# Running maxima by scalar columns on VectorE, h scaled out of PSUM, output in two alternating tiles

## The chip, the core and the metric

The kernel runs on one core of a Trainium2 chip. A core has a matrix engine (TensorE, "PE" in the profile; its weight loads are "PEld"), three engines for elementwise work (VectorE "DVE", ScalarE "ACT", GpSimd "POOL") and a queue that only issues transfers (SyncE "SP"). Each works through its own list of instructions in order, and they wait for one another by semaphores. SBUF is the working memory with 128 partitions; TensorE writes into PSUM, which has eight banks per partition. The metric is the device time of one execution in microseconds (us); the median of three is compared.

## The reference, cut to what matters

Two stages are chained: attention through 32 inducing points, and a channel mix. x has 4 batches of 12608 tokens of 128 channels.

```python
def mab(q, kv):
    s = scale * (q @ kv.transpose(0, 2, 1))
    s = s - s.max(-1, keepdims=True)
    a = np.exp(s)
    a /= a.sum(-1, keepdims=True) + 1e-09
    return a @ kv
h = mab(I, x)                  # 32 inducing points attend to all tokens of a batch
y = mab(x, h)                  # each token attends to the 32 rows of h
y_prev = y shifted by one token, zeros first
xk = mu_k * y + (1 - mu_k) * y_prev
xr = mu_r * y + (1 - mu_r) * y_prev
k = np.maximum(xk @ w_k, 0)    # 128 -> 1024
v = k * k @ w_v                # 1024 -> 128
out = sigmoid(xr @ w_r) * v
```

The first `mab` needs a maximum over all 12608 tokens for each of the 32 inducing points. The kernel takes it as a running maximum over blocks.

## The kernel before, in words

A batch is cut into 24 groups of 512 tokens and one of 320; four groups make a block of 2048 tokens. `Q = 4`, `M = 32`, `P = 128`, `G = 512`.

**Stage A** (`stage_a`, one call per block and batch, for batches 1 to 3) computes the first attention. The four groups of a block lie in the four quarters of the partitions: the scores of 32 inducing points for group i stand on partitions 32i to 32i+31. So the row maximum `mx` (L364) has four values per inducing point, one in each quarter, and they have to meet and be the same in all four before the exponentials. `common` (L367) does this with a TensorE matmul (L371) whose stationary operand is `mx` broadcast to 128 columns and whose moving operand is the identity: afterwards every partition holds all 128 values along its row, in PSUM bank "b". `running` (L375) adds a mask `apart` that is 0 where a column belongs to the same inducing point and about -3e38 elsewhere (L377), and reduces the row together with the previous running maximum (L380); L382 scales it to the bias of the exponential. The tail block (`tail`, the sixth) first joins the maximum of the 320 last tokens (L370), and L418 adds the tail's sum.

**`combine`** ends stage A of a batch: `weights` makes the normalising factors, `hfin` (L515) multiplies them in, copies the result from PSUM bank "b" to SBUF as `hT` (L519), and `mixed` (L510) makes four scalings of it (L513), by mu_k, 1 - mu_k, mu_r and 1 - mu_r. `wpack` multiplies these into w_k and w_r on TensorE (L555), so that the channel mix works directly on the 32 attention weights of a token, packed four times (high and low parts) into 128 rows. For batch 0 the same functions run in `head()`, with the first two scalings; the two for mu_r run in unit 0 (`mixed_r`), and the weights go through `wpart` (L537).

**Stage B** (`stage_b`) computes a block's second softmax (VectorE and ScalarE) through PSUM bank "b" until L660 has read it, and spreads its high and low parts `ah` and `al` into the groups' tiles `R` by transfers from SP (L670).

**The channel mix** (`Group`) takes a group in four units of 256 columns of w_k: `up` (L779, L781: four matmuls), `square` (L791 VectorE; L796, L797 ScalarE; L799 GpSimd, the low part `kl` of the squares), `down` (L810: six matmuls, four units later, `LAG`). `zgate` makes the sigmoid, `gate` (L815) multiplies. `store` (L817) transposes a group into the output tile `ot` (L826); there is one tile of four groups, and after the fourth group four transfers of 256 KB go out from SP (L833). The transpose of the next group has to wait until they have landed. The last four full groups of batch 3 are sent one by one.

The order of the work is written out by hand: the main loop runs over 400 units, and at each unit runs the functions that `at(n, f)` (end of the unit) and `soon(n, f)` (behind the unit's `up`, ahead of `square`) put there. Each function issues its instructions to the ends of the engines' lists, so an instruction waits behind all that its engine was given before. Stage A's block j of the next batch begins at unit 12 j of the present one (for batch 1, 4 later), with the scores at t + 9 and the common maximum at t + 11; stage B's block j + 1 begins at 12 j + 1 and spreads from its tenth unit on; `combine` begins at 72. Units are 2.3 to 3.9 us long in the trace.

Of the kernel before, what the change touches and what calls it, by code (L numbers as in the profile page):

```python
# [8 lines left out]
F32 = mybir.dt.float32  # L9
# [10 lines left out]
def kernel(  # L20
# [16 lines left out]
    Q = 4  # L37
# [6 lines left out]
    UC = 2  # L44
    LAG = 4
    NU = FC // UC
    assert NBLK == 7 and C == P and M * Q == P and F % 1024 == 0 and TAIL % Q == 0
# [15 lines left out]
    def pb_tile(bank=None):  # L63

        return pb.tile([P, G], F32, name="pb_" + (bank or next(banks)))
# [13 lines left out]
    wr_sb = const.tile([P, C], F32, name="wr_sb")  # L79
    wv_sb = mp.tile([P, Q * G], F32, name="ot", bufs=1)[:, :F].rearrange("p (c d) -> p c d", d=C)  # L80

# [59 lines left out]
    stack_f = stack.rearrange("p i m -> p (i m)")  # L141
    apart = const.tile([P, P], F32, name="apart")

    def constants():
        for dst, src in ((omuk, muk), (omur, mur)):
            nc.vector.tensor_scalar(out=dst, in0=src, scalar1=-1.0, scalar2=1.0,
                                    op0=ALU.mult, op1=ALU.add)
        nc.vector.tensor_reduce(out=stack[:, 0, :], in_=ident.rearrange("p (i m) -> p m i", i=Q),
                                op=ALU.add, axis=AX.X)
        for i in range(1, Q):  # L150
            nc.vector.tensor_copy(out=stack[:, i, :], in_=stack[:, 0, :])
        nc.vector.tensor_scalar(out=apart, in0=stack_f, scalar1=-1.0, scalar2=3.0e38, op0=ALU.add, op1=ALU.mult)

# [160 lines left out]
    def stage_a(b, j, at, t):  # L314
# [4 lines left out]


        S = batches[b]
# [45 lines left out]
        def common():  # L367
            ps = pb_tile("b")
            if tail:
                nc.vector.tensor_tensor(out=L["mx"], in0=L["mx"], in1=L["mxt"], op=ALU.max)  # L370
            nc.tensor.matmul(out=ps[:, :P], lhsT=L["mx"].broadcast_to([P, P]), rhs=ident,  # L371
                             start=True, stop=True)
            L["cp"] = ps

        def running():  # L375
            mk = S.mk if j > 0 else sm.tile([P, P + 1], F32, name="mkr", bufs=2)
            nc.vector.tensor_tensor(out=mk[:, :P], in0=L["cp"][:, :P], in1=apart, op=ALU.add)  # L377
            S.mk = sm.tile([P, P + 1], F32, name="mkr", bufs=2)
            L["mx"] = S.mk[:, P:P + 1]
            nc.vector.tensor_reduce(out=L["mx"], in_=mk[:, :P + (j > 0)], op=ALU.max, axis=AX.X)  # L380
            L["nb"] = sm.tile([P, 1], F32, name="nb")
            nc.vector.tensor_scalar(out=L["nb"], in0=L["mx"], scalar1=-scale, scalar2=None, op0=ALU.mult)  # L382

# [29 lines left out]
        def sums():  # L413
            if j > 0:
                nc.vector.tensor_scalar(out=S.sum, in0=S.sum, scalar1=L["al"], scalar2=L["ss"],
                                        op0=ALU.mult, op1=ALU.add)
            if tail:
                nc.vector.tensor_tensor(out=S.sum, in0=S.sum, in1=L["sst"], op=ALU.add)  # L418

# [30 lines left out]
        at(t + 9, scores)  # L450
        soon(t + 11 + tail, common)
        at(t + 11 + tail, running)
# [18 lines left out]
    def combine(b, at=None, t=0):  # L471
# [38 lines left out]
        def mixed(*parts):  # L510
            for nm, mu in parts:
                h4 = L["h4"][nm] = sm.tile([P, P], F32, name="h4" + nm, bufs=1)
                nc.vector.tensor_scalar(out=h4, in0=L["h"], scalar1=mu, scalar2=None, op0=ALU.mult)  # L513

        def hfin():  # L515
# [4 lines left out]
            S.hT = h[:, :M]  # L520
            L["h"] = h
            L["h4"] = {}
            mixed(("k0", muk), ("k1", omuk))
            if not ahead:
                mixed(("r0", mur), ("r1", omur))
            S.W = [wp.tile([P, WF], F32R, name=f"W{s}") for s in range(2)]
# [52 lines left out]
        if ahead:  # L579
            return maxes, weights, hfin, wpart, lambda: mixed(("r0", mur), ("r1", omur))  # L580
        at(t + 9, weights)
# [171 lines left out]
    class Group:  # L753
# [63 lines left out]
        def store(self):  # L817

            g, w = self.g, self.w
            if g == NG - 1:  # L820
                self.S.ot = st.tile([P, G], F32, name="aT")
            elif g % Q == 0:
                self.S.ot = out_tile()
            ot = self.S.ot
            o = (g % Q) * G
            nc.vector.transpose(out=ot[:, o:o + w], in_=self.oT)  # L826
            span = 1 if self.b == B - 1 and g // Q == NBLK - 2 else Q
            if g % span == span - 1 or g == NG - 1:
                o0 = (g % Q - g % span) * G
                t0 = (g - g % span) * G  # L830
                dst = out[self.b, t0:t0 + o - o0 + w, :].rearrange("(s q) (j d) -> j q s d", q=M, d=M)
                for i in range(Q):
                    nc.sync.dma_start(out=dst[i], in_=ot[M * i:M * (i + 1), o0:o + w]  # L833
                                      .rearrange("q (s d) -> q s d", d=M))

    def out_tile():
        return mp.tile([P, Q * G], F32, name="ot", bufs=1)

# [40 lines left out]
    ab = [stage_a_head(j) for j in order_h]  # L879
    maxes, weights, hfin, wpart, mixed_r = combine(0)  # L880
    work = []
# [63 lines left out]
    def soon(n, f):  # L945
        early.setdefault(n, []).append(f)

    def start():
# [9 lines left out]
        def gate_bank(s):  # L958
            if s == 0:
# [9 lines left out]
             wa[1][2], wb[0][1], hi1, lo1, wb[0][2]])  # L969
        at(0, mixed_r)  # L970
        for f in (wb[1][0], wb[1][1]):
# [102 lines left out]
```

## Time and profile before

| | us |
|---|---|
| median of 3 runs | 1164.9 (1164.0 to 1166.22) |
| time of the profiled execution | 1164.7 |
| its span | 1162.9 |
| TensorE busy | 1117.1 |
| VectorE busy | 933.2 |
| ScalarE busy | 970.9 |
| GpSimd busy | 947.7 |

The profile is of one execution. "Span" runs from its first to its last instruction. A page shows busy times, 40 equal slices of the span with the busy share in tenths, the TensorE clock that was granted, the chain of work that ended last, groups of instructions, and transfers. Further views list who waited for whom, single instructions in order of time, and busy times of stretches. "L371" is line 371 of the kernel. An instruction's name gives its output and inputs by the program's tile names; a transfer has the queue that issued it. A fp32 matmul shows as two passes, so 18 of them are 36 rows.

### The profile page before, as it was taken

Reading aid. Unit: us, or ns where it says so; the run is one execution under the profiler, and the core shown is the slowest. Engines: PE = TensorE matmul, PEld = TensorE weight load, DVE = VectorE, ACT = ScalarE, POOL = GpSimd, SP = SyncE. Lnnn points to the kernel's source line nnn. Section 1 sums busy time; section 2 is a strip of 40 time slices with the busy share of each in tenths; the row PEclk is TensorE's granted clock in tenths of the full one; section 3 lists DMA queues with packets and bytes.
Section 4 is the critical chain, followed back from the end, with each engine's and each line's share of the span. In section 5 each row is a group of like instructions: output and inputs, shape, how many; then the busy total and the mean of one; then the engine's idle time right before and its main releaser. Section 6 shows DMA issues by size and latency. Waiting matters only on the chain.

```text
span 1162.9 us, 17578 instructions
## 1 busy us (share of the span) xinstructions
PE 1117.1 (96%) x5746; PEld 836.6 (72%) x5746; DVE 933.2 (80%) x1259; ACT 970.9 (83%) x1107; POOL 947.7 (81%) x413
## 2 busy tenths in 40 slices
PE   6789999999999999999999999999999999999997
PEld 4466777776677777777768777677768777777886
DVE  5788888886878888888787889897787888877665
ACT  5488888887888888788978988888789888889996
POOL 1168888887787888888879888878878899999997
PEclk9999999999999999999999999999999999999999
DMA  9122654544226355465043553645204314432231
GB/s 295 42 50 64 130 120 112 102 117 81 44 56 134 105 106 123 108 133 120 5 77 77 117 124 105 133 98 122 45 18 79 63 34 73 73 64 46 43 46 34
DMA packets 273515, 102.31 MB, mean 88 GB/s; under 512 B 232816, under 2 KB 248336, under 8 KB 271120
## 3 DMA queue, kind: packets, MB, share of 16 engines
q1 hardware_dynamic: 273088, 101.17, 40.7%
q8 instruction: 46, 0.75, 0.3%
q14 instruction: 45, 0.37, 0.1%
q10 hardware_dynamic: 336, 0.02, 0.0%
HBM read 28.07 MB, written 25.82 MB: 46 GB/s over the span
## 4 chain that ended last, share of the span: by engine, by line
PE 65%; DVE 13%; ACT 8%; issue 5%; DMA 4%; SPq 4%; POOL 0%; DVEq 0%; ACTq 0%; POOLq 0%
PE ps_v L810 33%; PE ps_a L779 12%; PE ps_a L781 11%; DVE k_t L791 5%; ACT kh L796 2%; DMA out_dram<-ot 2%; PE pb_a L426 2%; ACT k_t L797 2%; PE ps_v L768 1%; SPq L833 1%; PE pb_b L616 1%; PE ps_v L769 1%; PE pb_a L361 1%; ACT L771 1%; ACT L633 1%
## 5 line engine op out<-in xcount | busy, mean ns | idle before, releaser
L799 POOL TENSOR_TENSOR kl<-k_t,kh 128x1024 fp32r<-128x1024 f32 (+2 forms) x400 | 939.0, 2375 | 175.8 <-ACT k_t L797 156.5
L791 DVE TENSOR_SCALAR k_t<-ps_a 128x1024 f32<-128x1024 f32 (+1 forms) x400 | 480.7, 1202 | 154.3 <-PE ps_a L781 143.5
L797 ACT ACTIVATE k_t<-k_t 128x1024 f32<-128x1024 f32 (+1 forms) x400 | 418.2, 1048 | 45.5 <-DVE kh L793 34.3
L796 ACT ACTIVATE kh<-k_t 128x1024 fp32r<-128x1024 f32 (+1 forms) x352 | 366.0, 1040 | 106.7 <-DVE k_t L791 56.1
L779 PE MATMUL ps_a<-R,W 128*128 128x512 f32 (+1 forms) x800 | 326.3, 408 | 6.7 <-DMA R<-al 3.4
L781 PE MATMUL ps_a<-R,W 128*128 128x512 f32 (+1 forms) x800 | 314.2, 393 | 0.0
L810 PE MATMUL ps_v<-kh,wvh 128*128 128x512 f32 (+1 forms) x800 | 252.2, 396 | 5.6 <-ACT rT L771 5.2
L810 PE MATMUL ps_v<-kh,wvl 128*128 128x512 f32 (+1 forms) x800 | 250.1, 394 | 0.0
L810 PE MATMUL ps_v<-kl,wvh 128*128 128x512 f32 (+1 forms) x800 | 250.0, 394 | 0.0
L779 PEld LDWEIGHTS ps_a<-R,W 128*128 128x128 f32 x800 | 151.4, 189 | 84.8 <-issue 20.7
L810 PEld LDWEIGHTS ps_v<-kh,wvh 128*128 128x128 f32 x800 | 147.9, 189 | 42.4 <-ACT rT L771 10.2
L810 PEld LDWEIGHTS ps_v<-kl,wvh 128*128 128x128 f32 x800 | 150.4, 189 | 35.8 <-POOL kl L799 0.3
L810 PEld LDWEIGHTS ps_v<-kh,wvl 128*128 128x128 f32 x800 | 150.3, 189 | 35.0
L781 PEld LDWEIGHTS ps_a<-R,W 128*128 128x128 f32 x800 | 151.3, 189 | 29.9
L826 DVE STREAM_TRANSPOSE ot<-oT 128x512 f32<-128x512 f32 x96 | 67.4, 702 | 12.0 <-DMA out_dram<-ot 11.2
L815 DVE TENSOR_TENSOR oT<-ps_v,rT 128x512 f32<-128x512 f32 (+1 forms) x100 | 66.6, 666 | 2.4 <-PE ps_v L810 0.2
L793 DVE SCALAR_TENSOR_TENSOR kh<-ps_a,k_t 128x1024 fp32r<-128x1024 f32 x48 | 58.8, 1225 | 5.4 <-PE ps_v L810 0.5
L771 ACT ACTIVATE rT<-ps_v 128x512 f32<-128x512 f32 (+1 forms) x99 | 57.3, 579 | 0.3
L333 DVE STREAM_TRANSPOSE xs<-xb 128x512 f32<-128x512 f32 x72 | 50.0, 694 | 1.8 <-DMA xb<-in_x_dram 1.6
L771 ACT ACT_TABLE_LOAD x31 | 39.8, 1283 | 0.6
L768 PE MATMUL ps_v<-R,W 128*128 128x512 f32 (+1 forms) x99 | 39.1, 395 | 0.1
L769 PE MATMUL ps_v<-R,W 128*128 128x512 f32 (+1 forms) x99 | 38.7, 391 | 0.0
(192 smaller groups left out, 642.3 us busy)
## 6 DMA issues: line engine op xcount, KB each, us to landing
out_dram<-ot SPq DMA_DIRECT2D x92, 256.0 KB, 4.3
xb<-in_x_dram SPq DMA_DIRECT2D x18, 1024.0 KB, 5.3
xt<-xs SPq DMA_DIRECT2D x288, 64.0 KB, 2.0
R<-ah SPq DMA_DIRECT2D x184, 64.0 KB, 2.0
R<-al SPq DMA_DIRECT2D x184, 64.0 KB, 2.0
kh<-in_x_dram SPq DMA_DIRECT2D x4, 512.0 KB, 7.0
kl<-in_x_dram SPq DMA_DIRECT2D x4, 512.0 KB, 6.3
xb<-in_x_dram SPq DMA_DIRECT2D x8, 256.0 KB, 5.5
```

The costliest lines, as they stand in the source:

```text
L768: nc.tensor.matmul(out=ps[:, :w], lhsT=S.W[0][:, F:WF], rhs=R[:, 1:w + 1], start=True, stop=False)
L771: nc.scalar.activation(out=self.rT, in_=ps[:, :w], func=AF.Sigmoid)
L779: nc.tensor.matmul(out=ps[:, c, :w], lhsT=S.W[0][:, cs], rhs=R[:, 1:w + 1], start=True, stop=False)
L781: nc.tensor.matmul(out=ps[:, c, :w], lhsT=S.W[1][:, cs], rhs=R[:, 0:w], start=False, stop=True)
L791: nc.vector.tensor_scalar(out=k, in0=self.ps[:, :, :w], scalar1=0.0, scalar2=None, op0=ALU.max)
L793: nc.vector.scalar_tensor_tensor(out=kh, in0=self.ps[:, :, :w], scalar=0.0, in1=k, op0=ALU.max, op1=ALU.mult)
L796: nc.scalar.activation(out=kh, in_=k, func=AF.Square)
L797: nc.scalar.activation(out=k, in_=k, func=AF.Square)
L799: return lambda eng, a, z: eng.tensor_tensor(out=kl[:, :, a:z], in0=k[:, :, a:z], in1=kh.bitcast(F32)[:, :, a:z], op=ALU.subtract)
L810: nc.tensor.matmul(out=self.v, lhsT=wt[:, fc, :], rhs=kk[:, c, :], start=(fc == 0 and n == 0), stop=(fc == FC - 1 and n == 2))
L815: nc.vector.tensor_tensor(out=self.oT, in0=self.v, in1=self.rT, op=ALU.mult)
L826: nc.vector.transpose(out=ot[:, o:o + w], in_=self.oT)
```

## The change

- **Maxima.** `common` no longer uses TensorE or PSUM. A VectorE `tensor_scalar` takes the maximum of partitions 0 to 63 with a column of scalars that lies on partitions 64 to 127; a second one takes the maximum of the lower 32 of these with the upper 32, and with the old running maximum where there is one. `running` copies the 32 results to the second quarter and the 64 then to the other half, and scales them. All these have one element per partition. The mask `apart` is gone. `common` moves from ahead of `square` in unit t + 11 to the end of unit t + 10 (one later for the tail block).
- **Two sums and maxima of the tail block** (L370, L418) become `tensor_scalar` with a column.
- **h's scalings** (L513) read the PSUM tile instead of its copy in SBUF; for batch 0 all four run in `hfin`, and `mixed_r` goes.
- **Output.** `ot` is a tile of two groups (`UO = 2`) with two buffers, in the same space; four transfers of 128 KB go out after every second group. The last four full groups of batch 3 still go one by one. w_v's staging area in the head, which shares the tile, fits one buffer.

```diff
+    UO = 2
-    wv_sb = mp.tile([P, Q * G], F32, name="ot", bufs=1)[:, :F].rearrange("p (c d) -> p c d", d=C)
+    wv_sb = mp.tile([P, UO * G], F32, name="ot")[:, :F].rearrange("p (c d) -> p c d", d=C)
-    apart = const.tile([P, P], F32, name="apart")
-        nc.vector.tensor_scalar(out=apart, in0=stack_f, scalar1=-1.0, scalar2=3.0e38, op0=ALU.add, op1=ALU.mult)
...
         def common():
-            ps = pb_tile("b")
+            v, half = nc.vector, P // 2
             if tail:
-                nc.vector.tensor_tensor(out=L["mx"], in0=L["mx"], in1=L["mxt"], op=ALU.max)
-            nc.tensor.matmul(out=ps[:, :P], lhsT=L["mx"].broadcast_to([P, P]), rhs=ident,
-                             start=True, stop=True)
-            L["cp"] = ps
+                v.tensor_scalar(out=L["mx"], in0=L["mx"], scalar1=L["mxt"], scalar2=None, op0=ALU.max)
+            mh = sm.tile([half, 1], F32, name="mh", bufs=1)
+            v.tensor_scalar(out=mh, in0=L["mx"][:half], scalar1=L["mx"][half:], scalar2=None, op0=ALU.max)
+            L["mx"] = sm.tile([P, 1], F32, name="mkr", bufs=2)
+            if j > 0:
+                v.tensor_scalar(out=L["mx"][:M], in0=mh[:M], scalar1=mh[M:], scalar2=S.mrun[:M],
+                                op0=ALU.max, op1=ALU.max)
+            else:
+                v.tensor_scalar(out=L["mx"][:M], in0=mh[:M], scalar1=mh[M:], scalar2=None, op0=ALU.max)
         def running():
-            mk = S.mk if j > 0 else sm.tile([P, P + 1], F32, name="mkr", bufs=2)
-            nc.vector.tensor_tensor(out=mk[:, :P], in0=L["cp"][:, :P], in1=apart, op=ALU.add)
-            S.mk = sm.tile([P, P + 1], F32, name="mkr", bufs=2)
-            L["mx"] = S.mk[:, P:P + 1]
-            nc.vector.tensor_reduce(out=L["mx"], in_=mk[:, :P + (j > 0)], op=ALU.max, axis=AX.X)
+            v, half = nc.vector, P // 2
+            v.tensor_copy(out=L["mx"][M:half], in_=L["mx"][:M])
+            v.tensor_copy(out=L["mx"][half:], in_=L["mx"][:half])
             L["nb"] = sm.tile([P, 1], F32, name="nb")
-            nc.vector.tensor_scalar(out=L["nb"], in0=L["mx"], scalar1=-scale, scalar2=None, op0=ALU.mult)
+            v.tensor_scalar(out=L["nb"], in0=L["mx"], scalar1=-scale, scalar2=None, op0=ALU.mult)
...
-                nc.vector.tensor_tensor(out=S.sum, in0=S.sum, in1=L["sst"], op=ALU.add)
+                nc.vector.tensor_scalar(out=S.sum, in0=S.sum, scalar1=L["sst"], scalar2=None, op0=ALU.add)
...
-        soon(t + 11 + tail, common)
+        at(t + 10 + tail, common)
...
-                nc.vector.tensor_scalar(out=h4, in0=L["h"], scalar1=mu, scalar2=None, op0=ALU.mult)
+                nc.vector.tensor_scalar(out=h4, in0=L["hp"], scalar1=mu, scalar2=None, op0=ALU.mult)
...
-            L["h"] = h
+            L["hp"] = ps[:, :P]
             mixed(("k0", muk), ("k1", omuk))
-            if not ahead:
-                mixed(("r0", mur), ("r1", omur))
+            mixed(("r0", mur), ("r1", omur))
...
-            elif g % Q == 0:
-                self.S.ot = out_tile()
+            elif g % UO == 0:
+                self.S.ot = mp.tile([P, UO * G], F32, name="ot")
-            o = (g % Q) * G
+            o = (g % UO) * G
-            span = 1 if self.b == B - 1 and g // Q == NBLK - 2 else Q
+            span = 1 if self.b == B - 1 and g // Q == NBLK - 2 else UO
...
-        at(0, mixed_r)
```

More of the change, by code (lines that the diff above doesn't have):

```diff
@@ L579, in combine @@
         if ahead:
-            return maxes, weights, hfin, wpart, lambda: mixed(("r0", mur), ("r1", omur))
+            return maxes, weights, hfin, wpart
         at(t + 9, weights)
@@ L821, in store @@
                 self.S.ot = st.tile([P, G], F32, name="aT")
-            elif g % Q == 0:
-                self.S.ot = out_tile()
+            elif g % UO == 0:
+                self.S.ot = mp.tile([P, UO * G], F32, name="ot")
             ot = self.S.ot
-            o = (g % Q) * G
+            o = (g % UO) * G
             nc.vector.transpose(out=ot[:, o:o + w], in_=self.oT)
-            span = 1 if self.b == B - 1 and g // Q == NBLK - 2 else Q
+            span = 1 if self.b == B - 1 and g // Q == NBLK - 2 else UO
             if g % span == span - 1 or g == NG - 1:
-                o0 = (g % Q - g % span) * G
+                o0 = (g % UO - g % span) * G
                 t0 = (g - g % span) * G
@@ L834, in store @@
                                       .rearrange("q (s d) -> q s d", d=M))
-    def out_tile():
-        return mp.tile([P, Q * G], F32, name="ot", bufs=1)
     def run(th):
@@ L879 @@
     ab = [stage_a_head(j) for j in order_h]
-    maxes, weights, hfin, wpart, mixed_r = combine(0)
+    maxes, weights, hfin, wpart = combine(0)
     work = []
```

## The prediction

> **What bounds the kernel now.** I read the page first (busy times, slices, chain), then the waits, then the timeline at the places the change touches.
>
> ```profile
> PE 1117.1 (96%) x5746; PEld 836.6 (72%) x5746; DVE 933.2 (80%) x1259; ACT 970.9 (83%) x1107; POOL 947.7 (81%) x413
> PE   6789999999999999999999999999999999999997
> PE 65%; DVE 13%; ACT 8%; issue 5%; DMA 4%; SPq 4%; POOL 0%; DVEq 0%; ACTq 0%; POOLq 0%
> ```
>
> TensorE is full except in the first three slices and the last, and has 65% of the chain. What can be gained is TensorE work that disappears, TensorE waits that disappear, and a shorter head. VectorE has room: the waits show it idle for TensorE.
>
> ```profile
> DVE k_t L791 <- PE ps_a L781: 143.5, 177, 2.8
> DVE ot L826 <- DMA out_dram<-ot: 11.2, 6, 2.7
> PE pb_b L371 <- DVE mx L370: 4.0, 3, 1.8
> PEld pb_a L426 <- DVE e L405: 2.3, 3, 1.2
> PE ps_a L779 <- DMA R<-al: 3.4, 2, 2.1
> PE pb_b L371 <- DVE al L660: 2.2, 3, 1.1
> PEld pb_a L555 <- DVE h4k L513: 2.0, 3, 0.7
> PE pb_a L555 <- DVE al L565: 1.4, 3, 0.5
> ```
>
> Columns: us in total, times, longest. Two of these waits stand at the removed matmul (L371: 4.0 for the tail blocks' maximum L370, 2.2 for the bank "b" that the softmax ahead of it still holds until L660), two behind h's scalings (L513).
>
> **Part 1: the matmul of the maxima goes.** From the timeline (start, length, line, operation, idle time before it in brackets), one ordinary instance of 18 and the worst; the last row is of the view by windows:
>
> ```profile
> 170.72 0.38 PE L371 MATMUL pb_b<-ident,mx 128*128 128x128 f32 x2
> 170.86 0.71 PE L810 MATMUL ps_v<-kh,wvh 128*128 128x512 f32 x2
> ...
> 274.46 0.40 PE L781 MATMUL ps_a<-R,W 128*128 128x512 f32 x1
> 276.66 0.46 PE L371 MATMUL pb_b<-ident,mx 128*128 128x128 f32 x2 [1.80 <-DVE mx L370]
> ...
> 277.00:281.00 4.00, 4.00 (x13) 3.17 (x12) 1.29 (x4) 2.11 (x2) 1.98 (x2) 0.57 0.08 17
> ```
>
> Slot: the next matmul starts 0.14 us after L371 (170.86 - 170.72), so 18 x 0.14 = **2.5 us** of TensorE. Waits: 4.0 + 2.2 = **6.2 us**, all at a matmul that no longer exists. After the wait of 1.80 us TensorE's granted clock over the 4 us from 277 to 281 is 0.57 (the third number from the end), while TensorE is busy throughout: 4 x (1 - 0.57) = **1.7 us** of delay, which goes with the wait. What had been late there was VectorE, for two reasons, and both leave with this change: a wait for the output tile (part 3), and L370 itself, a one-element operation that took 1.95 us because, as I read it, its two SBUF inputs met a GpSimd operation (timeline of VectorE and GpSimd; rows with three durations give min/median/max of a line):
>
> ```profile
> 274.56 1.95 DVE L370 TENSOR_TENSOR mx<-mx,mx 128x1 f32<-128x1 f32 x1
> ...
> 63.98 2.36 POOL L799 TENSOR_TENSOR kl<-k_t,kh 128x1024 fp32r<-128x1024 f32 x1 [0.22 <-ACT k_t L797]
> ...
> 65.10 0.14 DVE L595 CAST R<-R 128x1 fp32r<-128x1 f32 x1
> ...
> 65.60 0.77 DVE L719 TENSOR_SCALAR sm<-sm 128x8 f32<-128x8 f32 x1
> ...
> L382 DVE TENSOR_SCALAR nb<-mkr x18: 153/154/157, 103.5 to 829.9; 128x1 f32<-128x1 f32 x18
> L415 DVE TENSOR_SCALAR sum<-sum,alpha,ss x15: 251/255/269, 157.6 to 845.1; 128x1 f32<-128x1 f32 x15
> L377 DVE TENSOR_TENSOR mkr<-pb_b,apart x18: 271/280/280, 102.9 to 829.2; 128x128 f32<-128x128 f32 x18
> L380 DVE TENSOR_REDUCE mkr<-mkr x18: 286/288/289, 103.2 to 829.5; 128x1 f32<-128x129 f32 x15, 128x1 f32<-128x128 f32 x3
> ```
>
> Inside one GpSimd operation (63.98 to 66.34) a copy of one element per partition took its 0.14 us while an SBUF operation of eight elements lasted until 66.37, when GpSimd ended. L382 (18 times, at most 157 ns) and L415 (15 times, two scalar columns, at most 269) were never held. All new operations have one element per partition, so I price each at L382's 0.15 and a gap of 0.04 (as between hT and L700 in part 2): five cost 0.95 us a block, against 0.28 + 0.29 + 0.15 = 0.72 for L377, L380 and L382, which they replace. The extra 0.23 x 18 = 4.1 us lie under VectorE's 143.5 us of waiting; uncovered they would cost 4.1. Unknown is what a scalar column or a copy across quarters costs, since no row has one: bounds are 0.14 (L595) and GpSimd's end, up to 2.36 each (the slower rival below). I take the lower, nearest by size. L418, the tails' other small sum, changes as L370 does; no wait of TensorE hangs on it: 0.
>
> The Trainium skill, "SBUF — State Buffer", section "Who interferes with whom", says that copies and operations with a scalar can enter a two-port mode and then block on GpSimd until it ends; read so, the new copies are held. The rows of L595 and L382 speak against it for one element.
>
> **Part 2: h's scalings read PSUM.**
>
> ```profile
> 307.46 0.30 DVE L513 TENSOR_SCALAR h4k<-hT,muk 128x128 f32<-128x128 f32 x1
> 307.68 2.43 DVE L513 TENSOR_SCALAR h4k<-hT,omuk 128x128 f32<-128x128 f32 x1
> ...
> 302.88 9.47 POOL L799 TENSOR_TENSOR kl<-k_t,kh 128x1024 fp32r<-128x1024 f32 x4
> ...
> 313.81 0.19 PEld L779 LDWEIGHTS ps_a<-R,W 128*128 128x128 f32 x1 [0.50 <-DVE k_t L791]
> ...
> L513 DVE TENSOR_SCALAR h4k<-hT,omuk x4: 281/2421/2429, 48.6 to 857.8; 128x128 f32<-128x128 f32 x4
> L513 DVE TENSOR_SCALAR h4r<-hT,mur x4: 286/2404/2416, 58.3 to 860.1; 128x128 f32<-128x128 f32 x4
> ...
> L638 DVE TENSOR_SCALAR sm<-pb_b x27: 160/174/176, 89.5 to 1073.8; 128x16 f32<-128x16 f32 x23, 128x3 f32<-128x3 f32 x4
> ```
>
> Two of the four scalings last as long as a GpSimd operation (9.47 / 4 = 2.37) in three batches, and 0.28 in batch 0, where GpSimd rests. From PSUM, L519's copy of the same shape took 0.30 us (below), and L638, an operation from PSUM into SBUF, at most 176 ns in all 27. So VectorE gets back 2 x 2.13 = 4.3 us per batch. TensorE was late for it by the 2.0 (for h4k) + 1.4 (for L565 behind it) of the waits, and by some 0.3 of the 0.50 per batch at 313.81: **4.3 us**. Bounds: 2.0 and 12.8 (all of 3 x 4.3).
>
> In batch 0 all four now stand in the head, and they read the bank "b" that the first scores (L700) write next:
>
> ```profile
> 48.03 0.30 DVE hT L519
> 48.33 0.04 issue
> 48.37 0.64 PE pb_b L700 x16
> ```
>
> Those lines are of the chain (start, length). L700 today follows hT at once; now it waits for four more reads, 0.22 us apart like 307.46 and 307.68, the last of 0.29: 0.04 + 3 x 0.22 + 0.29, **+1.0 us**. Nothing hides it, since the two scalings that leave unit 0 lay beside other waits. Bounds 0.5 and 1.2.
>
> **Part 3: two output tiles.** VectorE's 11.2 us of waiting for the output transfers vanishes, since a tile is reused two groups later. Part of it was the late L660 and L370 counted above; what else TensorE paid I read at L426's 2.3 us (e is late behind the transpose): half of it, **1.2 us**, bounds 0 and 2.3. The price is on the DMA queue: 92 stores of 256 KB become 184 of 128 KB, and the pair's transposes and stores also go ahead of whatever SP has next.
>
> ```profile
> out_dram<-ot SPq DMA_DIRECT2D x92, 256.0 KB, 4.3
> out_dram<-ot SPq DMA_DIRECT2D x16, 64.0 KB, 1.9
> L833 SPq DMA_DIRECT2D out_dram<-ot x108: 315/988/1946, 125.5 to 1158.2; - x108
> ...
> 96.61 0.70 DVE L826 STREAM_TRANSPOSE ot<-oT 128x512 f32<-128x512 f32 x1
> ...
> 101.25 0.51 SPq L670 DMA_DIRECT2D R<-al  x1
> 102.44 0.58 SPq L670 DMA_DIRECT2D R<-al  x1
> ```
>
> A set of four halves should hold SP between 4 x 0.5 (near the 64 KB ones) and 4 x 0.99 us; I take 2.6. SP waits most of the time for VectorE and ScalarE, and the new store of unit 13, behind the transpose that ends at 97.3, holds it until 99.9, before the al pieces that TensorE waits for (issued at 101.25 and 102.44) are ready. But the two maxima of unit 14 now go ahead of that al: **+0.4 us**. For stores and displaced waits elsewhere I allow **+1.0 us**, an estimate between 0 and 5 (two sets in the way).
>
> **Sum.** Gain 2.5 + 6.2 + 1.7 + 4.3 + 1.2 = 15.9; cost 1.0 + 0.4 + 1.0 = 2.4; net -13.5 us. Against this execution's own time of 1164.7 (span 1162.9), 0.2 under the median of 1164.9, that gives 1151.2; on the median 1151.4. I take 1151.3.
>
> **Rivals.** *Stores in the way* (14%): twice as many stores sit ahead of R's pieces, which are late already (3.4 us at two places). With one set of 2.6 us in the way at both, the net is -13.5 + 5.2 = -8.3: 1156.4. For it: SP works in order. Against: the set fits before 101.25 at the one place. The Trainium skill, "SBUF — State Buffer", section "The DMA setup-cost knee", puts about 2 us of fixed cost on each transfer and advises few large ones, which speaks for this rival. The 1.9 us of a 64 KB store agrees; but nothing waits for a store here except L826.
>
> *Waits come back* (12%): TensorE runs ahead and meets the next late engine; half of 6.2 + 1.2 + 4.3 returns: -13.5 + 5.9 = -7.6, 1157.1. For it: GpSimd's 2.37 us per unit of work leaves little to spare where TensorE does nothing else. Against: GpSimd is idle 19%.
>
> *Short operations are held* (8%), the slower side: copies across quarters, or the maxima with a foreign column, block on GpSimd like L719. The first then waits half of 2.36 on average, the second a whole one: 3.5 us a block, 18 times. Part 2's 4.3 us of VectorE cost TensorE 4.3 / 3 = 1.4; at that rate 3.5 cost 1.2, so 18 x 1.2 = 21 us, and 1151.3 + 21 = 1172.3. It turns slower once a block loses 13.5 / 18 = 0.75 us of TensorE, 2.3 us of VectorE. For it: eight elements were held. Against: 33 of 33 one-element operations were not.
>
> That part 2 doesn't do what it says, and PSUM sources are held too, would give back 4.3 (1155.6); L638 speaks against it, and it lies inside the range.
>
> **Chances.** The forecast holds 66%. A measurement can tell about 0.2%, 2.3 us. Forecast, stores and returned waits all lie under 1162.6, but each may be worse than priced: faster 0.87, same 0.05, slower 0.08. Range 1145 (part 2 at twice its price, 4.3 more; part 3 at 2.3, 1.1 more; no allowance, 1.0 more) to 1159 (returned waits, with 1.5 to spare); the slower rival is left out.
>
> **What would show it.** Right: L371 gone, no long idle time of TensorE near those units; all L513 under 0.4 us; no wait of L826 for out_dram; new one-element rows at 0.14 to 0.2; L700 about 1 us later behind hT. Wrong: copies of 1 to 2.4 us; R's spreads issued behind L833, with L779's waits for R grown; or k_t's waits for ps_a turning into TensorE idle time elsewhere.

## The result, and the profile after

The changed kernel takes 1146.39 us (median of 4 runs, 1145.99 to 1148.12) against 1164.45 for the kernel before, timed beside it: a ratio of 0.985 with a 95% interval of [0.9832, 0.9868], 18.1 us less. The profiled execution took 1146.12 us, its span is 1144.2.

The page after, in the parts that answer to those shown of before (busy times, slices, chain by engine):

```profile
PE 1101.5 (96%) x5710; PEld 830.8 (73%) x5710; DVE 918.0 (80%) x1294; ACT 971.8 (85%) x1107; POOL 948.4 (83%) x413
PE   6778999999989999999999999999999999999997
PE 79%; DVE 9%; ACT 7%; issue 3%; DMA 1%; SPq 0%; DVEq 0%; ACTq 0%
```

TensorE has 36 rows fewer (18 matmuls of two passes) and is busy 15.6 us less. Its share of the chain went from 65% to 79%, and what VectorE, the stores and SP had there shrank: DMA from 4% to 1%, SP from 4% to 0%.

The waits after (us in total, times, longest):

```profile
DVE k_t L792 <- PE ps_a L782: 145.1, 177, 2.7
PE ps_a L780 <- DMA R<-al: 4.7, 2, 2.4
DVE xs L331 <- DMA xt<-xs: 1.5, 1, 1.5
```

All waits that stood at the removed matmul are gone, with those behind h's scalings and VectorE's 11.2 us for the output transfers. The wait for the pieces of `al` grew from 3.4 to 4.7 us, and one for the transfers from `xs` is new.

The new operations, line by line (min/median/max in ns, first and last start):

```profile
L371 DVE TENSOR_SCALAR mh<-mx x18: 207/208/211, 102.3 to 811.4; 64x1 f32<-64x1 f32 x18
L374 DVE TENSOR_SCALAR mkr<-mh,mkr x15: 258/260/262, 139.8 to 811.6; 32x1 f32<-32x1 f32 x15
L377 DVE TENSOR_SCALAR mkr<-mh x3: 200/201/202, 102.5 to 642.5; 32x1 f32<-32x1 f32 x3
L381 DVE COPY mkr<-mkr x18: 142/143/144, 104.6 to 813.8; 32x1 f32<-32x1 f32 x18
L382 DVE COPY mkr<-mkr x18: 147/147/150, 104.8 to 813.9; 64x1 f32<-64x1 f32 x18
L384 DVE TENSOR_SCALAR nb<-mkr x18: 153/154/156, 105.0 to 814.1; 128x1 f32<-128x1 f32 x18
L515 DVE TENSOR_SCALAR h4k<-pb_b,muk x4: 341/343/344, 49.6 to 840.7; 128x128 f32<-128x128 f32 x4
L515 DVE TENSOR_SCALAR h4k<-pb_b,omuk x4: 341/344/344, 49.8 to 840.9; 128x128 f32<-128x128 f32 x4
```

None is ever held: the longest of each is within 4 ns of its shortest. A column of scalars from other partitions costs about 50 ns more than a constant (L371 and L377 at 0.20 to 0.21 against L384's 0.15), a second one another 60 (L374). The scalings from PSUM take 0.34 us in all batches.

For the place of the gain I took the start of each of the 400 units (its first matmul of L779, in the new kernel L780) in both traces and looked where the difference jumps. Negative is time gained:

| place | units | us |
|---|---|---|
| head, with the first units | 0 to 7 | +1.6 |
| batch 1's first block | 16, 17 | +2.25 |
| blocks where L371 had waited | 28, 77 and 78, 160, 173, 260, 273 | -0.7, -3.8, -1.4, -1.6, -1.6, -1.6: -10.7 |
| the other eleven L371 | 40, 52, 64, 112, ... | -0.22 each: -2.4 |
| behind h's scalings | 88 to 90, 184 to 186, 284 to 286 | -1.7, -1.6, -1.6: -5.0 |
| behind e (L426) | 59, 146, 246 | -0.8, -1.0, -0.8: -2.7 |
| TensorE's clock, batch 1 to 2 | 101, 102 | -1.5 |
| a new wait | 206 | +1.4 |
| all others, each under 0.4, and the end | | -1.7 |
| sum: 1144.2 - 1162.9 | | -18.7 |

**The head.** The chain of waits after (start, length):

```profile
49.37 0.29 DVE hT L521
49.66 0.52 DVE h4k L515 x2
50.18 0.52 DVE h4r L515 x2
50.70 0.04 DVE R L592
50.73 0.02 issue
50.75 0.64 PE pb_b L701 x16
```

The first scores (L701) start 1.38 us after hT starts; before it was 0.34. That is the +1.0 that was forecast. The rest of the +1.6 belongs to these two executions: hT itself starts 1.34 us later here (49.37 against 48.03; in `no_maxima` below, with the same scalings, 48.02), and the kernel before lost clock among its first units, at 55.48 and 65.72, where the new one did not.

**Batch 1's first block**, and the new wait at unit 206, in the timeline (start, length, engine, line, operation, idle time before it in brackets):

```profile
98.92 2.73 SPq L834 DMA_DIRECT2D out_dram<-ot  x4
...
102.28 0.21 DVE L371 TENSOR_SCALAR mh<-mx 64x1 f32<-64x1 f32 x1
102.52 0.20 DVE L377 TENSOR_SCALAR mkr<-mh 32x1 f32<-32x1 f32 x1
102.75 0.69 DVE L661 TENSOR_TENSOR al<-pb_b,ah 128x512 fp32r<-128x512 f32 x1
...
103.60 0.55 SPq L671 DMA_DIRECT2D R<-al  x1
...
104.84 0.58 SPq L671 DMA_DIRECT2D R<-al  x1
...
107.01 0.77 PE L780 MATMUL ps_a<-R,W 128*128 128x512 f32 x1 [2.38 <-DMA R<-al]
...
623.06 0.71 DVE L331 STREAM_TRANSPOSE xs<-xb 128x512 f32<-128x512 f32 x1 [1.46 <-DMA xt<-xs]
...
624.27 0.48 DVE L816 TENSOR_TENSOR oT<-ps_v,rT 128x320 f32<-128x320 f32 x1
...
624.80 0.50 PE L769 MATMUL ps_v<-R,W 128*128 128x512 f32 x1 [1.05 <-DVE oT L816]
```

The view by windows, behind the wait (the stretch, busy times by engine; the granted clock is the third number from the end):

```profile
107.00:110.00 3.00, 2.99 (x7) 2.43 (x8) 0.83 (x1) 0.00 (x0) 3.00 (x2) 0.50 0.37 87
```

The two maxima stand ahead of `al`, as foreseen, and hold it by 0.47 us (102.28 to 102.75). TensorE's wait for it is 2.38 us, and over the next 3 us its clock is 0.50. That makes +2.25 where +0.4 was forecast: 0.84 at unit 16, where the wait is, and 1.41 at unit 17, where the clock is halved. The last three rows of the timeline are the new wait at unit 206: a transpose that waits for transfers stands ahead of the gate's product on VectorE, and TensorE waits for that.

### The profile page after: what moved, and what is told of

Same layout as the page of the kernel before. It is cut to its first block, busy times and chain, and to the rows that moved or that the text cites. A ratio compares the mean times of both kernels' runs of the same rounds, so it can differ in the third digit from the quotient of the medians.

```text
span 1144.2 us, 17672 instructions
## 1 busy us (share of the span) xinstructions
PE 1101.5 (96%) x5710; PEld 830.8 (73%) x5710; DVE 918.0 (80%) x1294; ACT 971.8 (85%) x1107; POOL 948.4 (83%) x413
## 4 chain that ended last, share of the span: by engine, by line
PE 79%; DVE 9%; ACT 7%; issue 3%; DMA 1%; SPq 0%; DVEq 0%; ACTq 0%
PE ps_v L811 40%; PE ps_a L780 15%; PE ps_a L782 13%; DVE k_t L792 3%; PE pb_b L617 2%; PE pb_a L428 2%; PE ps_v L769 2%; PE ps_v L770 2%; ACT kh L797 2%; PE pb_a L359 2%; ACT L772 1%; ACT L634 1%; ACT k_t L798 1%; DVE kh L794 1%; PE ps_a L227 1%
## 5 line engine op out<-in xcount | busy, mean ns | idle before, releaser
L780 PE MATMUL ps_a<-R,W 128*128 128x512 f32 (+1 forms) x800 | 326.0, 408 | 9.2 <-DMA R<-al 4.7
L811 PE MATMUL ps_v<-kh,wvh 128*128 128x512 f32 (+1 forms) x800 | 249.4, 393 | 5.3 <-ACT rT L772 4.7
L780 PEld LDWEIGHTS ps_a<-R,W 128*128 128x128 f32 x800 | 150.9, 189 | 86.2 <-issue 23.1
L770 PE MATMUL ps_v<-R,W 128*128 128x512 f32 (+1 forms) x99 | 38.7, 391 | 0.0
```

The source lines that it names most:

```text
L780: nc.tensor.matmul(out=ps[:, c, :w], lhsT=S.W[0][:, cs], rhs=R[:, 1:w + 1], start=True, stop=False)
L811: nc.tensor.matmul(out=self.v, lhsT=wt[:, fc, :], rhs=kk[:, c, :], start=(fc == 0 and n == 0), stop=(fc == FC - 1 and n == 2))
```

## The experiments

Two theories were tested against each other and against rivals: that each part earns what its place in the trace says, and that something else (short operations held, the stores) decides. All kernels compute the whole reference. The kernel before was timed beside each group and lay at 1163.5 to 1164.5.

### Each part alone

`maxima_alone` is the kernel before with the change's `common` and `running`, their places in the order and the tail's sums; `scalings_alone` with h's scalings; `tiles_alone` with the two output tiles. Their diffs are those parts of the change's diff.

> The kernel before with the maxima on VectorE alone (tail sums and the earlier place of common included); scalings and output tile as before. Theory (the gain is TensorE time at the places of the removed matmul): 18 slots of 0.14 us, the steps of 6.9 us at five places and of 3.8 us at unit 77 with its slow clock, less 0.5 for al: up to 12.7 us under before, 1152; since VectorE still waits for the output tile (11.2 us), one to four of these may come back: 1152 to 1156. Rival (the next late engine takes over): less than half, 1158 or more.

> The kernel before with h's scalings out of PSUM alone (all four of batch 0 in the head). Theory: VectorE gets 4.3 us back in each of three batches, TensorE 4.2 us in all at the units around the weights, against 1.0 us more in the head: 3 us under before, 1161 to 1162; all scalings at 0.34 us. Rival (the stall is hidden by TensorE's lead of four units): 1164 to 1166.

> The kernel before with two output tiles of two groups alone. Theory: VectorE's waits for the tile vanish, and with them what TensorE lost there: 2.7 us at the three matmuls with the transposed exponentials, 3.7 us at the three maxima that wait for al, 1 to 2 us at the first tail: 6 to 8 us under before, 1157 to 1159. The parts alone then add up to more than the whole change (about 23 against 18 us), since the waits at the maxima need only one of the two changes to go. Rival (transfers in the way): no gain, 1163 to 1167, with longer waits for R; the parts add up to 18 or less.

| | median, us | ratio to before |
|---|---|---|
| maxima alone | 1172.09 | 1.0064 [1.0044, 1.0085] |
| scalings alone | 1158.53 | 0.9947 [0.993, 0.9963] |
| tiles alone | 1155.43 | 0.9919 [0.99, 0.9938] |

The scalings earn 6.0 us, twice what was expected of them, and the tiles 9.1, a little more than expected. But the maxima, which should have brought the most, *cost* 7.6. The waits of maxima alone, and its page's row on the stores (KB each, us from issue to landing):

```profile
DVE ot L828 <- DMA out_dram<-ot: 28.3, 12, 4.8
```

```profile
out_dram<-ot SPq DMA_DIRECT2D x92, 256.0 KB, 5.2
```

VectorE's operations for the maxima were as short here as in the whole change. What grew is the time for the output transfers: 28.3 us in 12 waits instead of 11.2 in 6, since a store of 256 KB landed in 5.2 us instead of 4.3. Nothing in the edit touches a store. One thing does: it takes the mask `apart` (512 bytes a partition) and most of the `mkr` tiles away, and the tiles behind them move. In the addresses that the compiled programs give, the output tile starts at byte 165376 of each partition before (a multiple of 128), and at 163872 with the maxima alone and in the whole change, 32 past a multiple of 128.

### The address by itself

`before_shifted` is the kernel before with 32 unused bytes behind a small tile, so that the output tile starts at 165408; `before_shifted_64` has 64 of them (165440). `maxima_aligned` and `after_aligned` are maxima alone and the whole change with 96 unused bytes (163968, a multiple of 128 again).

```diff
# before_shifted (before_shifted_64: P + 16)
-            L["e1x"] = sm.tile([P, P], F32, name="mk", bufs=1)
+            L["e1x"] = sm.tile([P, P + 8], F32, name="mk", bufs=1)[:, :P]
...
# maxima_aligned, after_aligned
-            mh = sm.tile([half, 1], F32, name="mh", bufs=1)
+            mh = sm.tile([half, 25], F32, name="mh", bufs=1)[:, :1]
```

> The kernel before, nothing changed but one small tile (mk) 32 bytes wider, so that the output tile starts 32 past a multiple of 128 bytes (165408). Theory: stores of 256 KB land in 5 us or more, VectorE's waits for the output tile grow from 11 to 25 or 30 us, and the time rises by 8 to 20 us: 1172 to 1184. Rival (address is nothing): 1164.5 within 2.5, stores at 4.3 us.

> The kernel before with the small tile mk 64 bytes wider, so that the output tile starts 64 past a multiple of 128 bytes (165440). Every stored piece is 128 bytes. If what counts is that a piece begins at a multiple of 64 bytes, stores take 4.3 us and the time stays at 1164.5 within 2.5; if it has to be 128 (a piece must not cross such a boundary), stores take 5.2 us and the time is near the 1181 of the tile 32 past a multiple.

> The maxima alone, as in the run before, with one small tile (mh) 96 bytes wider, so that the output tile starts again at a multiple of 128 bytes (163968; without that the smaller maxima tiles moved it to 163872, 32 past one; before it stood at 165376, a multiple of 128). Theory (the output tile's start address slowed the stores from 4.3 to 5.2 us, and VectorE's waits for the one tile ate the gain of the maxima): stores of 256 KB land in 4.3 us again, VectorE waits about 11 us for them, and the time is 9 to 13 us under before, 1152 to 1156. Rival (the maxima's place in VectorE's order makes the waits, the address is nothing): 1170 to 1174, stores at 5.2 us.

> The changed kernel with the same 96 bytes, both output tiles at multiples of 128. Theory: stores of 128 KB land in 2.7 us as with the tiles alone, instead of 3.3; nothing but SP's order waits for them with two tiles, so 0 to 3 us under the changed kernel: 1143.5 to 1146.5. Rival (address is nothing): 3.3 us and 1146.4 within 1.

| | median, us | ratio to before | a store lands in, us |
|---|---|---|---|
| before | 1163.52 | 1 | 4.3 (256 KB) |
| before, 32 bytes on | 1181.0 | 1.0149 [1.0128, 1.017] | 5.2 (256 KB) |
| before, 64 bytes on | 1182.75 | 1.0164 [1.015, 1.0178] | 5.2 (256 KB) |
| maxima aligned | 1156.95 | 0.9941 [0.9924, 0.9958] | 4.5 (256 KB) |
| whole change | 1146.39 | 0.985 [0.9832, 0.9868] | 3.3 (128 KB) |
| whole change, aligned | 1144.26 | 0.9835 [0.9811, 0.9858] | 2.7 (128 KB) |

Unused bytes alone make the kernel before 17.5 us slower. Three views of it, with 32 bytes: the page's transfers, the waits, and the stores' line (min/median/max in ns that an issue held SP):

```profile
out_dram<-ot SPq DMA_DIRECT2D x92, 256.0 KB, 5.2
...
R<-al SPq DMA_DIRECT2D x184, 64.0 KB, 2.0
```

```profile
DVE ot L826 <- DMA out_dram<-ot: 26.9, 12, 4.4
...
PE pb_b L371 <- DVE al L660: 7.0, 3, 2.8
```

```profile
L833 SPq DMA_DIRECT2D out_dram<-ot x108: 315/1460/2947, 125.4 to 1173.9; - x108
```

An issue holds SP 1.46 us instead of 0.99, VectorE waits 26.9 us for the tile, and the late `al` then costs TensorE 7.0 us at the matmul of the maxima instead of 2.2. The other transfers of the main loop kept their times, also those into `R`, whose tiles lie behind the widened one and moved with the output tile (2.0 us as before); so did the long operations of VectorE, ScalarE and GpSimd. So the maxima were right all along: with the address mended they bring 6.6 us by themselves. One tile still leaves its wait there, larger than before since TensorE comes sooner:

```profile
DVE ot L828 <- DMA out_dram<-ot: 15.1, 8, 3.5
```

With two tiles nothing waits for a store, and so the whole change carried the slow address unseen. Mending it moves the median by 2.1 to 2.6 us (the second figure with the later run of the same kernel, below), which the intervals don't separate from nothing; the landing times they do.

The Trainium skill, "DMA: Bandwidth & Descriptors", section "How a descriptor splits into AXI transactions", says that a read begins at a multiple of 256 bytes, and that a piece that starts past one fetches the bytes ahead of it too. The stored pieces are 128 bytes. By that rule, as an estimate, each lies within one such stretch of 256 bytes when the tile starts at a multiple of 128, and every second one straddles two when it starts 32 or 64 past: 1.5 transactions a piece instead of 1. The runs agree in that 32 and 64 cost the same, that 163968 (a multiple of 128 but not of 256) is about as good as 165376 (a multiple of both), and that the time rises; it rises by 5.2 / 4.3 = 1.2, not by 1.5. That this is the mechanism is argued; shown is the address.

### What the maxima bring, once the other two are in

`no_maxima` is the whole change with the matmul of the maxima kept (its output tile starts at 165376, a multiple of 128), to be set against `after_aligned`. `after_aligned_more` is `after_aligned` run once more.

> The kernel before with scalings out of PSUM and two output tiles (at 165376, a multiple of 128 bytes), but with the maxima's matmul as before. It gives what the maxima are worth once the other two are there, against the aligned changed kernel (1144.3). Theory: without the waits for al, which the tiles take away, the maxima are worth 18 slots of 0.14 us and the three tail waits of 1.5 to 2 us, 7 to 8 us: 1151 to 1153. Rival (the three parts add up: 1164.5 less 6.0 less 9.1): 1149 to 1150, the maxima worth 5; and if the maxima are worth nothing by themselves, 1144 to 1146.

> The kernel after with the output tile at a multiple of 128 bytes, taken once more beside the kernel before, to settle what the two-input operations of the tail block cost: with them the median was 1151.89 us, without them 1144.26 of 1142.2 to 1147.65, while the unit starts of the two traces differ by 1.0 to 1.1 us a batch, 3.1 in all. If the medians are right and the traces miss a part of it, the median stays at 1143 to 1146 us. If the traces are right, the first median came out low by chance and the median is now 1147.5 to 1150.

`no_maxima` took 1151.04 us, ratio 0.9901 [0.9883, 0.9919]; `after_aligned` 1144.26, and when run again 1143.76 (1142.54 to 1145.67), 0.9828 [0.9806, 0.985]. The maxima bring about 7 us on top of the other two. The waits without them:

```profile
PE pb_b L372 <- DVE mx L371: 3.4, 3, 1.1
```

The waits for `al` at that matmul have gone with the two tiles; those of the tail's maximum remain. The unit starts give 18 slots (0.22 each where no wait adds to it), and three jumps of 1.59 us at units 77, 173 and 273, which hold a slot each: 15 x 0.22 + 3 x 1.59 = 8.1 us, against 6.8 to 7.3 in the medians. Alone and aligned the three parts bring 6.0 + 9.1 + 6.6 = 21.7 us; together, aligned, 19.3 to 20.6. The difference is no larger than the noise of these medians; the wait for `al` at the matmul, which either of two parts removes, would account for it.

### The tail block's two-input operations

`tail_two_aligned` is `after_aligned` with the tail's maximum and sum as operations with two tensors again.

```diff
-                v.tensor_scalar(out=L["mx"], in0=L["mx"], scalar1=L["mxt"], scalar2=None, op0=ALU.max)
+                v.tensor_tensor(out=L["mx"], in0=L["mx"], in1=L["mxt"], op=ALU.max)
...
-                nc.vector.tensor_scalar(out=S.sum, in0=S.sum, scalar1=L["sst"], scalar2=None, op0=ALU.add)
+                nc.vector.tensor_tensor(out=S.sum, in0=S.sum, in1=L["sst"], op=ALU.add)
```

> The changed kernel, aligned, but the two tail operations (maximum and sum) have two SBUF inputs again. Theory: both rise to 1.2 to 2.0 us each in three batches, as they are held until GpSimd's operation ends, but no matmul stands behind the maximum any more, so TensorE loses 0 to 1 us per batch: 1144.3 to 1147. Rival (a held VectorE operation ahead of the maximum for k costs TensorE as much as it did at the matmul): 1.5 to 2 us per batch, 1149 to 1150.

It took 1151.89 us, 0.9902 [0.9884, 0.992]: 7.6 to 8.1 more, all that the maxima had brought, and above what the theory and its rival had expected. The two lines (min/median/max in ns), and in the timeline the wait that follows:

```profile
L369 DVE TENSOR_TENSOR mx<-mx,mx x3: 1890/1909/1912, 273.2 to 812.1; 128x1 f32<-128x1 f32 x3
...
L420 DVE TENSOR_TENSOR sum<-sum,sst x3: 1676/1678/1684, 291.9 to 830.7; 128x1 f32<-128x1 f32 x3
```

```profile
289.03 0.31 PE L411 MATMUL pb_b<-ident,s 128*80 128x128 f32 x1 [0.72 <-ACT s L400]
```

With scalars they take 0.20 and 0.21. The late maximum makes ScalarE's exponential late, and TensorE waits 0.7 us for it once a batch. In the unit starts (against the second `after_aligned`) the loss is 1.1 us a batch, 3.4 in all. The medians say more: the difference of the two ratios is 0.0067 or 0.0074, by which of the two `after_aligned` is taken, give or take about 0.003, so at least 4 us. In this pair of profiles the remainder lies at units 101 and 102 (1.6, TensorE's clock), 206 (0.5) and in the head and the end (1.3), places that also differ between two runs of the same kernel. The mean granted clock of the five timed executions points at the clock too: 0.991, against 0.996 and 0.995 of the two `after_aligned`; 0.003 to 0.005 of 1150 us is 4 to 5 us. Whether the held operations cause that is open.

### A copy of two elements

The slower rival said that the copies across quarters would be held. In the whole change they weren't; the test is to give them a second element.

```diff
-            L["mx"] = sm.tile([P, 1], F32, name="mkr", bufs=2)
+            L["m2"] = sm.tile([P, 2], F32, name="mkr", bufs=2)
+            L["mx"] = L["m2"][:, :1]
...
-            v.tensor_copy(out=L["mx"][M:half], in_=L["mx"][:M])
-            v.tensor_copy(out=L["mx"][half:], in_=L["mx"][:half])
+            v.tensor_copy(out=L["m2"][:M, 1:], in_=L["mx"][:M])
+            v.tensor_copy(out=L["m2"][M:half], in_=L["m2"][:M])
+            v.tensor_copy(out=L["m2"][half:], in_=L["m2"][:half])
```

> The changed kernel, but the running maximum is a tile of two equal columns: one more copy of one element makes the second column, and the two copies across quarters move two elements per partition in place of one. Theory (an operation between SBUF tiles is held until GpSimd's operation ends as soon as it has two elements, one element is not): the two copies last 1 to 2.4 us each on average, 3 us or more a block, and the time rises by 15 to 25 us to 1161 to 1171. Rival (what counts is not one element against two but the size, or copies across quarters are never held): copies stay at 0.15 us, the time at 1146 to 1147.

It took 1214.44 us, 1.0425 [1.0399, 1.0452]: 68 us above the change as made, more than expected. Its three copies, and the wait that carries the larger part of it:

```profile
L382 DVE COPY mkr<-mkr x18: 130/131/133, 104.0 to 879.5; 32x1 f32<-32x1 f32 x18
...
L383 DVE COPY mkr<-mkr x18: 1265/2320/2336, 104.2 to 879.7; 32x2 f32<-32x2 f32 x18
L384 DVE COPY mkr<-mkr x18: 161/2315/2332, 105.5 to 881.9; 64x2 f32<-64x2 f32 x18
```

```profile
PE ps_v L771 <- DVE oT L818: 38.7, 15, 3.0
```

The first line of its page:

```profile
PE 1129.4 (93%) x5710; PEld 841.9 (69%) x5710; DVE 984.3 (81%) x1312; ACT 970.4 (80%) x1107; POOL 947.5 (78%) x413
```

The copy of one element (L382) is free 18 times out of 18, those of two last up to a GpSimd operation. VectorE loses 2.11 + 1.84 - 0.29 = 3.7 us a block (means, less the 0.29 of the copies of one), and the kernel loses 68 / 18 = 3.8. That the two agree is chance, since the loss has two parts. TensorE's wait for the gate's product is 38.7 us, 2.2 a block. And its same 5710 rows take 1129.4 us instead of 1101.5, 27.9 more: behind the first unit this trace has 18 stretches of 3.41 us at half clock, the whole change one. So 2.2 of VectorE's 3.7 us are passed on, more than the third that I had taken from h's scalings, and the lower clock, for which the forecast had no term here, adds 1.6.

The Trainium skill, "VectorE: DVE Perf Modes", section "Mode 2×_2P", says that the mode with both ports needs an outermost dimension, other than one of length one, that is even (or odd and equal in source and destination). One element has none, two have. That fits these rows. The section cited in the prediction points to this condition, and the prediction left it out.

### The two losses mended

`best` is `after_aligned` with batch 0's scalings from the copy in SBUF again, the two for mu_r back in unit 0, and the maxima of batch 1's first block one unit later, behind `al`.

```diff
-        at(t + 10 + tail, common)
+        at(t + 10 + tail + (b == 1 and j == 0), common)
...
-                nc.vector.tensor_scalar(out=h4, in0=L["hp"], scalar1=mu, scalar2=None, op0=ALU.mult)
+                nc.vector.tensor_scalar(out=h4, in0=L["h"] if ahead else L["hp"], scalar1=mu, scalar2=None, op0=ALU.mult)
...
-            mixed(("r0", mur), ("r1", omur))
+            if not ahead:
+                mixed(("r0", mur), ("r1", omur))
...
+        at(0, mixed_r)
```

> The changed kernel with the output tiles at multiples of 128 bytes, batch 0's four scalings from the SBUF copy as before (the two for mu_r in unit 0 again), and the common maximum of batch 1's first block one unit later, behind al. Theory: the 1.0 us of the head and some of the 2.2 us at units 16 and 17 come back, beside the 0 to 3 us of the address: 1141 to 1145. Rival (these terms are hidden by the wait for R that follows in any case): no better than the aligned kernel, 1143.5 to 1146.5.

It took 1142.61 us (1141.46 to 1146.03), 0.9828 [0.9806, 0.985]: the lowest median of all, 3.8 under the change as made. The trace against that of the change shows the head 1.1 us and units 16 and 17 2.2 us shorter; 1.4 of the 2.2 is half clock behind the wait, which `after_aligned_more` doesn't have either, with the maxima still ahead of `al`. Against the kernel before the gain is clear. But its interval overlaps that of the change as made, and the two medians of `after_aligned`, 1144.26 and 1143.76, lie within its own runs: that the two repairs earn the 1.9 us that remain of the 3.3 in the traces cannot be told from the medians.

## Why the prediction was right, and where it was off

1151.3 us was forecast, between 1145 and 1159; 1146.4 was measured. Sign and mechanism held, and the gain was 18.1 us instead of 13.5. By the prediction's own terms, measured in the unit starts (span against span, -18.7):

| term | forecast | trace |
|---|---|---|
| 18 slots of L371 | -2.5 | -3.9 (18 x 0.22) |
| waits at L371, with the clock behind one | -7.9 | -9.4 (10.7 less 6 slots) |
| h's scalings | -4.3 | -5.0 (alone: -6.0 in the medians, the head's loss included) |
| e, behind the transposes (L426) | -1.2 | -2.7 |
| head | +1.0 | +1.6 |
| `al` behind the maxima | +0.4 | +2.5 (2.25 and its block's slot; 1.4 of it clock) |
| stores and displaced waits | +1.0 | +1.4 |
| not in the prediction | | -1.5 (clock), -1.7 (small ones) |

The gains that were sized too low (5.1 us together) and the two last entries (3.2) outweigh the costs that were sized too low (3.1). That the total came out as near as it did is in part luck.

- **The slot** was mis-sized: the next matmul's start, 0.14 us behind L371, isn't all that goes. 0.22 was measured wherever no wait added to it. Why it is more the runs do not show.
- **The waits at L371** were right in place and kind. They came out 1.5 us larger, as I read it because the waits view counts idle time only from the modelled end of the matmul before. The clock behind the wait of 1.80 us was no sure thing: 1.80 us is at the edge of what costs clock (see the clock, below). The three other kernels with this matmul and one output tile (`scalings_alone`, `before_shifted`, `before_shifted_64`) lose clock there too.
- **L426**: I took half of 2.3 us, from bounds of 0 and 2.3; 2.7 were gained, above the upper bound. The row is gone from the waits after, and with the two tiles alone as well: the whole of it was to be had, and the bound, from the same view as the last, was too low, I think in the same way.
- **The head** went as worked out, to 0.04 us in the chain. 0.34 us for a scaling from PSUM against the 0.29 taken is small beside it.
- **`al` behind the maxima** was seen, with its order on VectorE, but priced by VectorE's delay alone. The wait grew from 1.31 us (first row below) to 2.38, by 1.1, and the half clock behind it cost the other 1.4. The first part comes back in every trace with this order: 0.6 to 0.8 at unit 16, 0.6 in `after_aligned_more`, which waits 2.21 us there. The second does not: of the seven traces with the maxima ahead of this `al`, three have half clock behind the wait, and that one has not. I had charged clock only where it already stood in the trace, at 277, and not where the change made a wait longer.
- **The clock of -1.5 us** is none of the change's. Before, a wait of 2.08 us was followed by half clock; after, one of 2.31 us in the same unit was followed by full clock. The rows of before and, in the next two fences, of after, each with the view by windows in stretches of 3.41 us (TensorE's busy time is the second figure, the granted clock the third from the end):

```profile
104.56 0.47 PE L779 MATMUL ps_a<-R,W 128*128 128x512 f32 x1 [1.31 <-DMA R<-al]
...
344.54 0.46 PE L779 MATMUL ps_a<-R,W 128*128 128x512 f32 x1 [2.08 <-DMA R<-al]
```

```profile
342.20:345.62 3.42, 1.34 (x7) 0.92 (x6) 1.30 (x4) 2.70 (x4) 3.42 (x3) 1.00 0.43 102
345.62:349.03 3.41, 3.41 (x12) 3.02 (x11) 1.84 (x2) 1.85 (x2) 1.88 (x2) 0.50 0.27 57
```

```profile
340.56 0.47 PE L780 MATMUL ps_a<-R,W 128*128 128x512 f32 x1 [2.31 <-DMA R<-al]
```

```profile
335.41:338.82 3.41, 2.84 (x14) 2.08 (x12) 2.64 (x6) 3.35 (x7) 3.41 (x3) 1.00 0.18 41
338.82:342.23 3.41, 1.67 (x9) 1.52 (x10) 0.87 (x2) 1.92 (x3) 3.41 (x3) 1.00 0.48 114
342.23:345.65 3.42, 3.42 (x23) 2.29 (x21) 3.42 (x5) 2.46 (x3) 1.29 (x2) 1.00 0.28 60
```

  The fourteen traces show what decides. While the units run, half clock comes in stretches of 3.41 us (now and then two in a row), and in each trace they start whole multiples of 3.41 us apart: in that of before at 55.48, 65.72, 277.35 and 345.62, which is 3, 62 and 20 of them. Cut on this grid, from the first unit to the last matmul, the traces give 4431 stretches at full clock. All 46 with 1.85 us or more of TensorE idle (by the modelled ends of its matmuls) were followed by half clock, none of the 4374 with less than 1.72, and two of the 11 between. The 2.08 us of before lay whole in one stretch; of the 2.31 us of after, 0.57 fell into one and 1.74 into the next. Where the grid lies differs from execution to execution.

- **Stores in the way** did not decide, but it was close. The set at unit 13's transpose held SP for 2.73 us (2.6 was taken), two further transfers followed without a pause, and the first piece of `al` went out at 103.60, 0.16 us after it was ready (102.75 + 0.69 = 103.44). No transpose waits for a store any more.
- **Waits come back**: one did, at unit 206 (+1.4), where the rival had put 5.9.
- **Short operations held**: false for one element, as the 33 rows had said, and true for two, where the price per block was 3.8 us (2.2 of waiting, 1.6 of clock) and not 1.2.
- **What the prediction missed altogether** is that freeing SBUF moves the output tile. By itself that was worth 17.5 us in the kernel before, and 15 with the maxima alone (1172.09 against 1156.95), and only the two tiles of the same change kept it from being seen.

## What to carry to other kernels

A tile that is added, removed or resized moves all tiles behind it: when a part of a change goes the wrong way, look first at transfers that the edit doesn't touch, and compare their landing times and their tiles' start addresses. Time each part alone; a sum that comes out right can hide a part that went wrong and another that covered it. In these runs an operation of one element per partition whose second operand is a column of scalars was never held beside GpSimd; the same with two tensors took 1.7 to 1.9 us, and a copy of two elements up to 2.3, a whole GpSimd operation.

## What the runs showed of the hardware that I had not expected

- **Start address of a stored tile.** Pieces of 128 bytes from a tile that starts 32 or 64 bytes past a multiple of 128: 5.2 us to land 256 KB instead of 4.3, 3.3 for 128 KB instead of 2.7, and SP held 1.46 us an issue instead of 0.99.
- **TensorE's clock after a wait** goes by how much idle time falls into one stretch of a fixed grid of 3.41 us, not by the wait's length: of the stretches at full clock, those with 1.85 us or more of it were followed by half clock (46 of 46), those with less than 1.72 by full clock (4374 of 4374). A wait of 2.31 us that the grid cut in two cost no clock; one of 1.80 that it did not cut did.
- **One element against two**: 0.14 to 0.15 us against up to 2.34, for the same copy at the same place.
